# Gated attention and mixer-MLP kernel: W1 stored twice and split a step later, q and k written 16 dimensions outermost with two of three writes on ACT's queue, x and Wv issued earlier

## The chip, the core and the metric

The program runs on one core of a Trainium2 chip. The metric is the device time of one execution in microseconds. A measurement of this kernel can tell a change of about 1% from none.

## What is computed

x is 2048 tokens of 512 features in float32. Two branches are mixed by a gate per token:

```python
g = sigmoid((x * gate_w).sum(-1))
q, k, v = heads(x @ wqkv)                       # 32 heads of 16
p = softmax(where(0 <= i - j < 256, q k^T / 4, -1e9))
a = (p v) @ wo
b = gelu(layernorm(x) @ w1 + b1) @ w2 + b2      # 512 -> 1792 -> 512
out = g * a + (1 - g) * b
```

## The kernel before, in words

Every product in float32 accuracy is made of three fast products: an operand is split into h (a rounded copy, made by ACT in `copy`, line 98) and l (the rest, made by DVE or POOL in `lo_part`, line 95), and PE adds h h, l h and h l.

The program is written out in the order in which each engine runs it. SyncE (SP) issues all DMAs but one, in that order, and so do the compute engines with their instructions. `after(k, fn)` puts a piece of work k ticks later, and `tick()` runs what is due. Tiles called `t` come from one ring of raw buffers (12 in the first stage, 8 in the second); a new one waits until the last reader of the old one is done. Each DMA takes the next of eight semaphores in turn and waits until the DMA that had it last, eight issues earlier, has landed.

Stage 1 (to about 204 us) has 48 units, one a tick. A q/k unit (`qk_unit`, line 206) makes 128 rows of q or k, eight heads of 16 dimensions, for one of four chunks of 512 tokens: 12 matmuls into one of four PSUM banks, h by ACT, l by DVE, and three writes to HBM (line 222), h twice and l once, into a layout of 50 rows a head. A v unit (`v_unit`, line 225) makes 128 tokens of v and leaves them in SBUF. The first units are the q and k of heads 0 to 7 for chunks 0 to 2 (six units), then two v units, the q and k for chunk 3, and so on. The table `at(n, fn)` (lines 425 to 452) says before which unit the loads of x's chunks 2 and 3, of Wv (four tiles, `load_wv`), the gap rows (`gaps`, line 160), and the stacks of q and k for the first pair group are issued, and when the loaded tiles are split.

Stage 2 (about 204 to 757 us) runs over 8 groups p of four heads and 16 key blocks kb; one such step is one tick. A step makes the scores of a key block (`st_pair`: PE line 294, two exps by ACT line 296, masks by POOL line 298), the maxima for the group that comes next (`s_pair`: PE line 252, DVE lines 261 and 262), and in every other step the product with v (`pv`, PE line 309). Between these, `fill` puts matmuls of the first MLP layer (`mlp1_unit`, PE line 498), by a quota of 2.7 a half step. An MLP job is one tile of W1 (128 of the 1792 columns) with one half of the tokens. W1 has 14 such tiles; when the second job of tile f ends, `load_w1(f + 3)` issues the load of the next one:

```python
raws = [t2(), t2()]
for j, raw in enumerate(raws):
    sp.dma_start(raw, view(w1, [0, 2], [KT * 128, 64], [1, C], off=f * 64 * KT * 128 + j * C))
```

The 64 rows of W1 are needed in both halves of the 128 partitions, since two matmuls of 64 rows run side by side. `hi` (two copies on ACT) comes two ticks after the issue, `lo` (two subtractions, on DVE for the first three tiles, on POOL after) three ticks after. The first three tiles are loaded around the head of the stage, beside the second half of the normalised y (`load_y(1, 2, 1)`).

Stage 3 (from about 757 us) makes the second MLP layer (line 675) and the output projection (line 654).

Of the kernel before, what the change touches and what calls it, by code (L numbers as in the profile page):

```python
# [19 lines left out]
S = 2048  # L20
D = 512
H = 32
DH = 16
F = 1792
DT = D // 128
KT = D // 64
FT = F // 128
C = 512
NCH = S // C
NB = S // 128  # L30
NG = 4
HG = H // NG
# [11 lines left out]
def gated_mix_kernel(ctx, tc: tile.TileContext, xt, x2, wqk, wv, wo, xa, gw, w1, w2, b1, b2, out):  # L44
    nc = tc.nc
    dve, act, pool, pe, sp = nc.vector, nc.scalar, nc.gpsimd, nc.tensor, nc.sync
# [18 lines left out]
    def get(key, tag, bufs, shape, dt=F32):  # L65
        return left[key].tile(list(shape), dt, name=nm(tag), tag=tag, bufs=bufs)
# [3 lines left out]
    def t2(dt=F32, shape=(128, 512)):  # L70
        return get("work", "t", nt[0], shape, dt)
# [10 lines left out]
    def ps(tag, shape=(128, 512)):  # L82
        return left["psum"].tile(list(shape), F32, name=nm("ps_" + tag), tag=tag, bufs=banks[tag])
# [4 lines left out]
    def view(t, *ap, off=0):  # L88
        return bass.AP(tensor=t.tensor, offset=t.offset + off, ap=[list(x) for x in ap])

    def f32(t):
        return t.bitcast(F32)

    def lo_part(lo, src, hi, eng=dve):
        eng.tensor_tensor(out=lo, in0=src, in1=f32(hi), op=ALU.subtract)  # L95

    def copy(dst, src):
        act.activation(dst, src, AF.Copy)  # L98
# [4 lines left out]
    def after(k, fn):  # L103
        todo.setdefault(step[0] + k, []).append(fn)
# [34 lines left out]
    def x8():  # L139
        return get("x", "x8", 8, (128, 2048), F32R)  # L140

    def wt():
        return get("work", "w", 20, (128, 512), F32R)
# [16 lines left out]
    def gaps(g):  # L160
        for t in range(2):
            sp.dma_start(f32(view(qkd[g, t], [50 * S, HG], [S, 2], [1, S], off=48 * S)), f32(ks[0][112:128]))
# [15 lines left out]
    def load_wv(dt):  # L178
        raw = t2()
        sp.dma_start(raw, wv[dt])  # L180

        def rest():
            h, l = wt(), wt()
            copy(h, raw)
            lo_part(l, raw, h)
            wvs.append((h, l))

        return rest

    def load_x(c):  # L190
        raws = []
        for dt in range(DT):
            raws.append(t2())
            sp.dma_start(raws[dt], xt[c, :, dt * C:(dt + 1) * C])

        def rest(first=None):
            h, l = x8(), x8()
            for dt in range(DT):
                a, b = h[:, dt * C:(dt + 1) * C], l[:, dt * C:(dt + 1) * C]
                copy(a, raws[dt])  # L200
                lo_part(b, raws[dt], a, dve if c < 2 else pool)
                if dt == 0 and first:
                    first()
            xh.append(h)
            xl.append(l)

        return rest

    def qk_unit(g, t, c):
        d = qkd[g, t]  # L210
        o = ps("d")
        wh, wl = wq[g, t]
        n = 0
        for a, b in ((wh, xh[c]), (wl, xh[c]), (wh, xl[c])):
            for dt in range(DT):
                pe.matmul(o, a[:, dt * 128:(dt + 1) * 128], b[:, dt * C:(dt + 1) * C], start=n == 0, stop=n == 11)  # L216
                n += 1
        h, l = t2(F32R), t2(F32R)
        copy(h, o)
        lo_part(l, o, h)  # L220
        for k, s in ((0, h), (1 + t, h), (2 - t, l)):
            sp.dma_start(f32(view(d, [50 * S, HG], [S, DH], [1, C], off=k * DH * S + c * C)), f32(s))

    def v_unit(b):
        c, i = divmod(b, 4)
# [184 lines left out]
    wvr = []  # L410

    def QK(g, t, c):
        return lambda: qk_unit(g, t, c)
# [8 lines left out]
    def at(n, fn):  # L422
        plan.setdefault(n, []).append(fn)

    xs = {}
    at(0, lambda: xs.update({2: load_x(2)}))
    at(2, lambda: xs[2]())
    at(2, lambda: xs.update({3: load_x(3)}))
    at(4, lambda: xs[3]())
    for dt in range(DT):  # L430
        at(3 + dt // 2, lambda dt=dt: wvr.append(load_wv(dt)))
        at(5 + dt // 3, lambda dt=dt: wvr[dt]())
    for i in range(4):
        at(4 + i, lambda i=i: pool.memset(vs[:, 4 * i:4 * i + 4], 1.0))
    at(11, load_consts)
    for g in range(NG):
        at((1, 16, 20, 24)[g], lambda g=g: gaps(g))
    for c in range(NCH):
        at((4, 6, 8, 12)[c], lambda c=c: load_stacks(0, c))
    for i in range(NB):  # L440
# [23 lines left out]
    def load_w1(f):  # L464
        raws = [t2(), t2()]
        for j, raw in enumerate(raws):
            sp.dma_start(raw, view(w1, [0, 2], [KT * 128, 64], [1, C], off=f * 64 * KT * 128 + j * C))

        def hi():
            w1t[f] = get("work", "w1", 3, (128, 2, KT * 128), F32R)  # L470
            for j in range(2):
                copy(w1t[f][:, 0, j * C:(j + 1) * C], raws[j])

        def lo():
            for j in range(2):
                lo_part(w1t[f][:, 1, j * C:(j + 1) * C], raws[j], w1t[f][:, 0, j * C:(j + 1) * C], dve if f < 3 else pool)
            done.add(("w", f))

        after(2, hi)
        after(3, lo)  # L480

    jobs = [(0, 0), (1, 0), (0, 1), (1, 1)] + [(f, cp) for f in range(2, FT) for cp in range(2)]
    load_w1(0)
    load_y(1, 2, 1)
    after(1, lambda: load_w1(1))
    after(3, lambda: load_w1(2))

    def mlp1_unit(f, cp):
# [77 lines left out]
    for p in range(8):  # L566
        for kb in range(NB):
# [16 lines left out]
            if p == 7:  # L584
# [4 lines left out]
                if kb == 14:  # L589
                    for fn in ready:  # L590
                        fn()
                    t = x8()
# [93 lines left out]
    def item(n):  # L686
        return seq[n] if n < len(seq) else (0, -1)

    for n in range(len(seq)):
        tick()  # L690
        for k in (range(2, 4) if n == 0 else (n + 3,)):
            c, f = item(k)
# [4 lines left out]
        c, f = item(n + 1)  # L697
# [7 lines left out]
        c, f = seq[n]  # L705
# [11 lines left out]
def build():  # L717
    nc = bacc.Bacc("TRN2", target_bir_lowering=False, num_devices=1)

    def inp(name, shape):  # L720
        return nc.dram_tensor(name, list(shape), F32, kind="ExternalInput").ap()

    args = [inp("in_xt", (NCH, 128, DT * C)), inp("in_x2", (2, 128, KT * C)), inp("in_wqk", (NG, 2, 128, DT * 128)), inp("in_wv", (DT, 128, D)),
            inp("in_wo", (DT, 128, D)), inp("in_xa", (NB, 128, D)), inp("in_gw", (D,)),
            inp("in_w1", (FT, 64, KT * 128)), inp("in_w2", (FT, 128, D)), inp("in_b1", (128, FT)), inp("in_b2", (D,))]
    out = nc.dram_tensor("out", [NB, 128, D], F32, kind="ExternalOutput").ap()
    with tile.TileContext(nc) as tc:
        gated_mix_kernel(tc, *args, out)
    if not nc.is_finalized():
        nc.finalize()  # L730
    return nc
# [26 lines left out]
```

## Time and profile before

| | |
|---|---|
| median of 3 runs | 984.24 us (977.64 to 984.25) |
| the profiled execution | 978.83 us |
| its span | 977.1 us |
| PE (matmuls) busy | 775.8 us, 79% of the span |
| DVE busy | 516.1 us, 53% |
| ACT busy | 373.8 us, 38% |
| POOL busy | 303.0 us, 31% |
| mean granted TensorE clock | 0.896 of 2.4 GHz |

Times in the profile count from the start of the span. The busy times are means over stages with different limits, so a wait is read in its stage. A name such as `t<-in_w` is the tile written and the tensor read, with trailing digits left out (`in_w` is both `in_w1` and `in_w2`). "DMA" rows run from the issue to the landing.

### The profile page before, as it was taken

To read this page: it belongs to the slowest core of one execution; us is meant where nothing else is said; L and a number is where in the kernel's file an instruction comes from. 1 tells how busy PE (TensorE), PEld (TensorE's weight loads), DVE (VectorE), ACT (ScalarE), POOL (GpSimd) and SP (SyncE) were. 2 spreads that over 40 slices of the span, in tenths; PEclk is the share of its full clock that TensorE was granted. 3 is DMA by queue.
4 is the path that set the end of the run, shared out by engine and by line. 5 is a ranking of instruction groups with operands and counts; after the bars stand their busy time and mean duration, and the time that the engine had idled before them with its cause. 6 is when DMAs were issued, how large, how long until landed. Compare 5 with 4: busy or idle time off the path is not lost.

```text
span 977.1 us, 14415 instructions
## 1 busy us (share of the span) xinstructions
PE 775.8 (79%) x4832; PEld 534.6 (55%) x4832; DVE 516.1 (53%) x1087; ACT 373.8 (38%) x573; POOL 303.0 (31%) x597
## 2 busy tenths in 40 slices
PE   7498989914685669587696686876999699999998
PEld 5275657602453345354353454543556487888886
DVE  3126775602684347365384464654673566455544
ACT  4221112313553445354453454544556443222222
POOL 7500001702553435344363354443556000000000
PEclk9698989956797789797797988987999799999999
DMA  6776656633322233233223323332332755444442
GB/s 213 258 239 227 201 199 198 209 124 119 106 102 96 93 98 110 89 126 110 92 84 119 111 84 115 114 113 91 117 92 73 244 162 177 136 143 136 151 130 91
DMA packets 94741, 134.15 MB, mean 137 GB/s; under 512 B 13132, under 2 KB 38732, under 8 KB 94540
## 3 DMA queue, kind: packets, MB, share of 16 engines
q1 hardware_dynamic: 94524, 132.97, 41.4%
q8 instruction: 39, 0.64, 0.3%
q14 instruction: 34, 0.28, 0.1%
q10 hardware_dynamic: 144, 0.26, 0.1%
HBM read 78.91 MB, written 54.28 MB: 136 GB/s over the span
## 4 chain that ended last, share of the span: by engine, by line
PE 46%; DMA 29%; DVE 9%; SPq 5%; ACT 4%; POOL 3%; issue 3%; ACTq 0%; DVEq 0%; POOLq 0%
DMA t<-in_w 16%; PE ps_a L675 14%; PE ps_d L498 10%; PE ps_x L309 7%; PE ps_d L216 4%; PE ps_o L654 4%; PE ps_x L294 3%; PE ps_x L252 3%; DMA t<-in_xa 3%; DMA qk<-t 3%; DVE mx L262 2%; PE ps_d L231 2%; DVE ps_x L261 2%; ACT p L296 2%; DMA hp<-t 1%
## 5 line engine op out<-in xcount | busy, mean ns | idle before, releaser
L498 PE MATMUL ps_d<-x,w 64*128 64x512 f32 x1344 | 257.3, 424 | 21.1 <-ACT w L98 11.7
L298 POOL TENSOR_SCALAR_AFFINE_SELECT p<-p 128x256 f32<-128x256 f32 x480 | 188.0, 420 | 231.7 <-ACT p L296 228.1
L296 ACT ACTIVATE p<-ps_x 128x768 f32<-128x768 f32 (+2 forms) x256 | 192.9, 770 | 77.4 <-PE ps_x L294 63.0
L252 PE MATMUL ps_x<-k,q 62*128 62x384 f32 (+5 forms) x512 | 102.0, 380 | 109.2 <-ACT p L296 92.6
L261 DVE COPY_PREDICATED ps_x<-tri,ps_x 128x256 f32<-128x256 uint8 x224 | 94.9, 424 | 168.6 <-PE ps_x L252 168.0
L498 PEld LDWEIGHTS ps_d<-x,w 64*128 64x128 f32 x1344 | 146.3, 203 | 40.9 <-ACT w L98 12.8
L262 DVE TENSOR_REDUCE mx<-ps_x 128x2 f32<-128x512 f32 x224 | 155.1, 692 | 7.7
L675 PE MATMUL ps_a<-x,t 128*128 128x512 f32 x648 | 155.0, 397 | 0.1
L675 PEld LDWEIGHTS ps_a<-x,t 128*128 128x128 f32 x648 | 121.8, 188 | 30.2 <-DVE t L541 0.5
L252 PEld LDWEIGHTS ps_x<-k,q 48*128 48x128 f32 (+1 forms) x512 | 55.1, 197 | 138.2 <-ACT p L296 108.7
L294 PE MATMUL ps_x<-q,k 50*128 50x384 f32 (+5 forms) x512 | 105.4, 391 | 28.4 <-ACT p L296 22.3
L309 PE MATMUL ps_x<-p,v 128*32 128x384 f32 (+2 forms) x1024 | 101.3, 514 | 15.8 <-DVE mx L262 6.7
L294 PEld LDWEIGHTS ps_x<-q,k 50*128 50x128 f32 (+1 forms) x512 | 56.2, 197 | 94.2 <-issue 35.8
L216 PE MATMUL ps_d<-x,w 128*128 128x512 f32 x384 | 101.1, 420 | 6.1 <-ACT w L98 6.1
L216 PEld LDWEIGHTS ps_d<-x,w 128*128 128x128 f32 x384 | 75.8, 200 | 27.2 <-ACT w L98 6.1
L537 ACT ACTIVATE t<-t,b1s 128x512 f32<-128x512 f32 x56 | 39.5, 721 | 117.0 <-DMA t<-hp 111.4
L98 ACT ACTIVATE w<-t 128x512 fp32r<-128x512 f32 x40 | 25.2, 629 | 139.2 <-DMA t<-in_w 116.8
L98 ACT ACTIVATE t<-ps_x 128x512 f32<-128x512 f32 (+1 forms) x59 | 33.8, 573 | 112.1 <-PE ps_x L309 109.4
L309 PEld LDWEIGHTS ps_x<-p,v 128*32 128x32 f32 x1024 | 30.9, 116 | 67.9 <-issue 34.2
L95 DVE TENSOR_TENSOR t<-t,t 128x512 fp32r<-128x512 f32 x70 | 48.5, 692 | 30.8 <-ACT t L98 26.0
L319 POOL TENSOR_TENSOR t<-t,t 128x256 f32<-128x256 f32 x51 | 37.5, 736 | 87.4 <-ACT t L98 87.4
L231 PE MATMUL ps_d<-w,x 128*128 128x512 f32 x192 | 52.6, 425 | 14.1 <-ACT w L98 14.1
(66 smaller groups left out, 562.6 us busy)
## 6 DMA issues: line engine op xcount, KB each, us to landing
qk<-t SPq DMA_DIRECT2D x96, 256.0 KB
hp<-t SPq DMA_DIRECT2D x56, 256.0 KB
t<-hp SPq DMA_DIRECT2D x56, 256.0 KB
k<-qk SPq DMA_DIRECT2D x64, 196.0 KB
q<-qk SPq DMA_DIRECT2D x64, 196.0 KB
t<-in_w SPq DMA_DIRECT2D x42, 256.0 KB
osc<-t SPq DMA_DIRECT2D x64, 128.0 KB
t<-in_xt SPq DMA_DIRECT2D x16, 256.0 KB
```

The costliest lines, as they stand in the source:

```text
L98: act.activation(dst, src, AF.Copy)
L216: pe.matmul(o, a[:, dt * 128:(dt + 1) * 128], b[:, dt * C:(dt + 1) * C], start=n == 0, stop=n == 11)
L231: pe.matmul(o, x[:, a:a + 128], wvs[dt][k], start=n == 0, stop=n == 11)
L252: pe.matmul(o[:, e, :n], qs[pr][r:k, qb * 128:qb * 128 + 128], ks[pr][r:k, t0:t0 + n], start=True, stop=True)
L261: dve.copy_predicated(o[:, :, :128], tri, o[:, :, 256:384])
L262: dve.tensor_reduce(m, o[:, :, :256], mybir.AxisListType.X, ALU.max)
L294: pe.matmul(o[:, e, :w], ks[pr][r:k, kb * 128:kb * 128 + 128], qs[pr][r:k, kb * 128:kb * 128 + w], start=True, stop=True)
L296: act.activation(pt[:, :, :w], o[:, :, :w], AF.Exp, scale=0.25)
L298: pool.affine_select(out=pt[:, :, a:a + 128], in_=pt[:, :, a:a + 128], pattern=[[0, 2], [sgn, 128]], base=b, channel_multiplier=-sgn, comp ...
L309: pe.matmul(a[32 * h:32 * h + 32, odd * 128:odd * 128 + w], vs[:, kb, v:v + 32], pt[:, h, :w], start=not odd, stop=odd == 1, skip_group_ch ...
L498: pe.matmul(o[e], w[r:r + 64, k, kt * 128:kt * 128 + 128], y[r:r + 64, a:a + C], start=n == 0, stop=n == 23)
L675: pe.matmul(accs[c][b], x[:, b * 128:(b + 1) * 128], w, start=f == 0 and n == 0, stop=f == FT - 1 and n == 2)
```

## The change

W1 is handed over with its 64 rows repeated, so that a load reads 128 rows straight; the split of a W1 tile comes one tick later (3 and 4 ticks after the issue). The columns of the q and k weights are put in the order dimension, head, so that a unit's rows come out as 16 dimensions of 8 heads, and the writes have the 16 dimensions outermost; the bytes land where they did. The two writes of h are issued by ACT right behind its copy, the write of l by SP one tick later. x's chunk 3 is issued before unit 0 instead of 2, Wv's four tiles before units 1 and 2 instead of 3 and 4, and split before units 3 and 4 instead of 5 and 6; the gap rows of the first heads come a unit later.

```diff
-        for k, s in ((0, h), (1 + t, h), (2 - t, l)):
-            sp.dma_start(f32(view(d, [50 * S, HG], [S, DH], [1, C], off=k * DH * S + c * C)), f32(s))
+        for k in (0, 1 + t):
+            act.dma_start(f32(view(d, [S, DH], [50 * S, HG], [1, C], off=k * DH * S + c * C)), f32(h))
+        after(1, lambda: sp.dma_start(f32(view(d, [S, DH], [50 * S, HG], [1, C], off=(2 - t) * DH * S + c * C)), f32(l)))
...
-    at(2, lambda: xs.update({3: load_x(3)}))
+    at(0, lambda: xs.update({3: load_x(3)}))
     at(4, lambda: xs[3]())
     for dt in range(DT):
-        at(3 + dt // 2, lambda dt=dt: wvr.append(load_wv(dt)))
-        at(5 + dt // 3, lambda dt=dt: wvr[dt]())
+        at(1 + dt // 2, lambda dt=dt: wvr.append(load_wv(dt)))
+        at(3 + dt // 2, lambda dt=dt: wvr[dt]())
...
-        at((1, 16, 20, 24)[g], lambda g=g: gaps(g))
+        at((2, 16, 20, 24)[g], lambda g=g: gaps(g))
...
         for j, raw in enumerate(raws):
-            sp.dma_start(raw, view(w1, [0, 2], [KT * 128, 64], [1, C], off=f * 64 * KT * 128 + j * C))
+            sp.dma_start(raw, w1[f, :, j * C:(j + 1) * C])
...
-        after(2, hi)
-        after(3, lo)
+        after(3, hi)
+        after(4, lo)
...
-            inp("in_w1", (FT, 64, KT * 128)), inp("in_w2", (FT, 128, D)), inp("in_b1", (128, FT)), inp("in_b2", (D,))]
+            inp("in_w1", (FT, 128, KT * 128)), inp("in_w2", (FT, 128, D)), inp("in_b1", (128, FT)), inp("in_b2", (D,))]
...
     w1 = B_w1.reshape(KT, 64, FT, 128).transpose(2, 1, 0, 3).reshape(FT, 64, KT * 128)
+    w1 = np.concatenate([w1, w1], axis=1)
...
-        "in_wqk": f(A_wqkv[:, :2 * D].reshape(DT, 128, 2, NG, 128).transpose(3, 2, 1, 0, 4).reshape(NG, 2, 128, DT * 128)),
+        "in_wqk": f(A_wqkv[:, :2 * D].reshape(DT, 128, 2, NG, HG, DH).transpose(3, 2, 1, 0, 5, 4).reshape(NG, 2, 128, DT * 128)),
```

Line numbers from 222 on are higher by one after the change.

On SP near the start, before; `qk` is the q/k tensor in HBM, `in_xt` x, `in_wv` Wv:

```order
L194 DMA t_41_223<-in_xt 128x512
L194 DMA t_42_225<-in_xt 128x512
L194 DMA t_43_227<-in_xt 128x512
L194 DMA t_44_229<-in_xt 128x512
L222 DMA qk0_0_65<-t_46_244 8x16x512 x2
L222 DMA qk0_0_65<-t_47_245 8x16x512
L180 DMA t_48_251<-in_wv 128x512
L180 DMA t_49_253<-in_wv 128x512
L222 DMA qk0_1_66<-t_51_268 8x16x512 x2
L222 DMA qk0_1_66<-t_52_269 8x16x512
L180 DMA t_55_285<-in_wv 128x512
L180 DMA t_56_287<-in_wv 128x512
```

On SP near the start, after:

```order
L194 DMA t_33_171<-in_xt 128x512
L194 DMA t_34_173<-in_xt 128x512
L194 DMA t_35_175<-in_xt 128x512
L194 DMA t_36_177<-in_xt 128x512
L223 DMA qk0_0_65<-t_39_193 16x8x512
L180 DMA t_40_199<-in_wv 128x512
L180 DMA t_41_201<-in_wv 128x512
L223 DMA qk0_1_66<-t_44_217 16x8x512
L180 DMA t_47_233<-in_wv 128x512
L180 DMA t_48_235<-in_wv 128x512
```

Wv stood behind x's last chunk and the writes of four units (those of the first two stand above the piece shown); now the last chunk of x comes first of all, and one write of l from each of the first two units stands ahead of Wv.

On ACT near the start, after; before, these rows are the same without the two DMA rows, and the copies of x's third chunk (`x8_39` there) follow the second copy of `ps_d` at once:

```order
L98 ACTIVATE t_38_192<-ps_d_37_179 128x512
L222 DMA qk0_0_65<-t_38_192 16x8x512 x2
L98 ACTIVATE t_43_216<-ps_d_42_203 128x512
L222 DMA qk0_1_66<-t_43_216 16x8x512 x2
L98 ACTIVATE x8_45_223<-t_29_163 128x512
L98 ACTIVATE x8_45_223<-t_30_165 128x512
```

Each of the 32 q/k units now has two DMA issues in ACT's order between one copy out of PSUM and the next.

On ACT in stage 2 at the fourth tile of W1, before; `p` is an exp, `t<-ps_d` the copy that ends an MLP job, before the W1 load of that job, and `w1<-t` the copies of the loaded tile:

```order
L296 ACTIVATE p_405_2179<-ps_x_406_2180 128x2x256
L296 ACTIVATE p_405_2179<-ps_x_408_2194 128x2x256
L98 ACTIVATE t_411_2205<-ps_d_385_2045 128x512
L98 ACTIVATE t_415_2223<-ps_x_414_2214 128x512
L296 ACTIVATE p_416_2229<-ps_x_417_2230 128x2x128
L296 ACTIVATE p_416_2229<-ps_x_421_2252 128x2x128
L98 ACTIVATE w1_423_2270<-t_409_2201 128x512
L98 ACTIVATE w1_423_2270<-t_410_2202 128x512
```

The same place on ACT after:

```order
L98 ACTIVATE t_418_2239<-ps_d_387_2054 128x512
L297 ACTIVATE p_421_2258<-ps_x_422_2259 128x768
L297 ACTIVATE p_421_2258<-ps_x_426_2282 128x768
L98 ACTIVATE t_429_2308<-ps_x_428_2299 128x256
L297 ACTIVATE p_430_2312<-ps_x_431_2313 128x768
L297 ACTIVATE p_430_2312<-ps_x_433_2328 128x768
L98 ACTIVATE w1_438_2351<-t_416_2235 128x512
L98 ACTIVATE w1_438_2351<-t_417_2236 128x512
```

Between the end of the job that issues the load and the copies of the tile stand the exps of two steps instead of one.

## Rows read from the trace of the kernel before

**Rows 1.** The page, part 4: the chain that ended last, by line.
```profile
DMA t<-in_w 16%; PE ps_a L675 14%; PE ps_d L498 10%; PE ps_x L309 7%; PE ps_d L216 4%; PE ps_o L654 4%; PE ps_x L294 3%; PE ps_x L252 3%; DMA t<-in_xa 3%; DMA qk<-t 3%; DVE mx L262 2%; PE ps_d L231 2%; DVE ps_x L261 2%; ACT p L296 2%; DMA hp<-t 1%
```

**Rows 2.** Windows: length, busy (instructions) of PE, PEld, DVE, ACT, POOL; PEclk, DMA share, GB/s.
```profile
26.00:50.00 24.00, 9.91 (x29) 6.66 (x28) 3.92 (x6) 6.78 (x12) 12.55 (x8) 0.64 0.74 259
50.00:196.65 146.65, 131.79 (x544) 98.33 (x542) 88.97 (x213) 31.85 (x57) 21.48 (x16) 0.95 0.64 212
204.30:290.10 85.80, 49.73 (x352) 29.80 (x354) 42.04 (x83) 35.56 (x54) 31.82 (x63) 0.74 0.32 102
290.10:674.90 384.80, 278.46 (x2286) 171.38 (x2282) 205.33 (x464) 170.07 (x255) 170.73 (x375) 0.87 0.31 103
757.00:977.10 220.10, 208.38 (x900) 165.31 (x892) 120.31 (x202) 70.22 (x111) 2.12 (x5) 0.97 0.48 152
```

**Rows 3.** Waits, whole span: waiter, waited for; us in total, times, longest.
```profile
ACT w L98 <- DMA t<-in_w: 116.8, 28, 8.5
```

**Rows 4.** Timeline 307.5 to 326, SP and ACT: start, us, instruction, idle before.
```profile
309.99 1.09 SPq L467 DMA_DIRECT2D t<-in_w  x2
...
312.61 1.51 ACT L296 ACTIVATE p<-ps_x 128x768 f32<-128x768 f32 x2
317.76 0.63 ACT L98 ACTIVATE w<-t 128x512 fp32r<-128x512 f32 x1 [3.65 <-DMA t<-in_w]
323.02 0.63 ACT L98 ACTIVATE w<-t 128x512 fp32r<-128x512 f32 x1 [4.63 <-DMA t<-in_w]
```

**Rows 5.** Windows as in rows 2, three short stretches.
```profile
317.00:322.50 5.50, 0.00 (x0) 0.00 (x0) 0.00 (x0) 0.63 (x1) 0.00 (x0) 0.76 0.13 50
187.00:200.00 13.00, 8.27 (x37) 6.01 (x35) 4.40 (x8) 3.64 (x7) 5.45 (x4) 0.88 0.52 198
314.50:316.50 2.00, 1.49 (x14) 0.80 (x10) 1.71 (x3) 0.00 (x0) 0.53 (x2) 1.00 0.90 338
```

**Rows 6.** Windows of line 296 (the exps) alone: length, ACT busy (count), PEclk, DMA, GB/s.
```profile
683.20:736.20 53.00, 24.28 (x33) 1.00 0.35 109
290.10:674.90 384.80, 127.92 (x171) 0.87 0.31 103
262.60:285.50 22.90, 9.73 (x12) 1.00 0.33 109
204.30:290.10 85.80, 23.28 (x30) 0.74 0.32 102
```

**Rows 7.** Chain that ended last, in order of time, to 212 us: start, us, what.
```profile
0.80 4.07 DMA t<-in_xt
...
89.57 8.37 DMA t<-in_xa
...
200.03 5.46 DMA qk<-t
```

**Rows 8.** Groups by line and form: busy us, mean ns, idle before.
```profile
L95 POOL TENSOR_TENSOR w<-t,w 128x512 fp32r<-128x512 f32 x22 | 27.8, 1282 | 0.0
```

**Rows 9.** Timeline 0 to 60, as rows 4.
```profile
16.50 5.05 POOL L95 TENSOR_TENSOR x<-t,x 128x512 fp32r<-128x512 f32 x4 [2.67 <-ACT x L98]
17.80 4.74 SPq L222 DMA_DIRECT2D qk<-t  x3
...
27.89 1.32 SPq L180 DMA_DIRECT2D t<-in_wv  x2
...
32.17 1.49 SPq L180 DMA_DIRECT2D t<-in_wv  x2
...
36.44 1.45 PE L231 MATMUL ps_d<-w,x 128*128 128x512 f32 x2 [9.94 <-ACT w L98]
...
41.84 0.80 PE L231 MATMUL ps_d<-w,x 128*128 128x512 f32 x1 [3.94 <-ACT w L98]
```

**Rows 10.** Timeline 196 to 205, as rows 4.
```profile
204.31 0.81 ACT L296 ACTIVATE p<-ps_x 128x768 f32<-128x768 f32 x1 [8.06 <-DMA qk<-t]
```

## The prediction, made before the changed kernel ran

> **What bounds the kernel now.** I read the chain that ended last first: the largest DMA share in it is the load of W1 into its raw buffers [rows 1]. Then busy time by stretch [rows 2]. The last 220.10 us have PE busy for 208.38 and the change leaves them alone. The attention and first-MLP stage is the place: from 290.10 to 674.90 PE works 278.46 of 384.80 us. The table of waits says who is late: ACT waited 28 times for W1, 116.8 us in all, up to 8.5 us each [rows 3]. One such wait in order of time [rows 4]: SP issues both halves of a W1 tile at 309.99, ACT is done with the exps of its step at 314.12 (312.61 + 1.51), and the copies of the halves start at 317.76 and 323.02. ACT runs in order, so the exps behind the copies are late, and with them PE. Meanwhile [rows 5] from 317 to 322.5 the DMA engines are 0.13 busy and move 50 GB/s, which is two of sixteen; just before, under the writes of the MLP's results, they stood at 0.90 and 338 GB/s. So W1 is slow because nearly all of the engines do nothing. The q and k writes at the end of the first stage show the same at half: 0.52 busy and 198 GB/s for 13 us, eight of sixteen. The source agrees with both: W1's read has an outermost dimension of 2, the q/k write one of 8.
>
> A row shows the busy share, not the cause. The Trainium skill (DMA: Bandwidth & Descriptors, "Why a DMA increments its semaphore by 16 and not by 1") says that a DMA of SP or ACT runs on the largest number of engines up to 16 that divides the slowest dimension of both sides, and its rules name a leading broadcast of c copies as confined to c. The trace agrees at 2 and at 8; no row shows it for a write with 16 outermost. By the rule the time is the forecast below, without it the 912 of the second rival.
>
> **W1 in the steady stretch, 290.10 to 674.90.** It holds 171 exps, two a step, so 85 steps [rows 6], and eleven of the fourteen W1 tiles. Between 683.20 and 736.20 no W1 comes in and all else goes on: 33 exps, so 16 steps, in 53.00 us, 3.31 us a step, at a granted clock of 1.00 (2.4 GHz) where the long stretch has 0.87. If no copy waits any more, 85 x 3.31 = 281 us. Does it wait? The copies now stand one step further back, so ACT comes to them about 3.5 + 3.3 = 6.8 us after the second half was issued (that was near 310.5, and ACT stood free at 314.1). A 256 KB load of 128 rows landed in 4.07 us at the quiet start and in 8.37 us at the worst of the first stage [rows 7], both from the chain, and 50 GB/s turning into the 338 of rows 5 takes the two halves from 10.5 us of moving to 1.6. I take landed in time; at the worst 1.6 us are left per tile. What the clean stretch lacks is the split itself: two ACT copies of 0.63 us (rows 4) and two POOL subtractions of 1.28 us [rows 8]. They cost between nothing, beside PE, and 3.8 us in line; I take 1.3, near the ACT part, since the masks on POOL have a step of slack before PE's PV reads them. 11 x 1.3 = 14. So 384.8 - 281 - 14 = 90 us gained; bounds 384.8 - 281 = 104 and, with 3.8 + 1.6 each, 44.
>
> **W1 at the head of that stage, 204.30 to 290.10.** 30 exps, 15 steps in 85.80 us, clock 0.74; it holds three W1 tiles and the second half of y. The stretch 262.60 to 285.50 has y but no W1: 12 exps, six steps in 22.90 us, 3.8 a step. 15 x 3.8 = 57, and 3 x 1.3 = 4 for the splits: 61, a gain of 24. Bounds: 36 at 3.31 a step, and 0 if it is DVE's work on y, beside which it splits W1, that sets this stretch. The matmuls of the MLP also begin one step later, and the order has twelve more of them in the drain at the end: 278.46 / 2286 = 0.12 us each, 1 us lost.
>
> **The first stage.** Three things. Wv first: PE waits 9.94 and 3.94 us for it [rows 9], since its loads stand on SP behind x's last chunk and behind writes, issued at 27.89 and 32.17. Now the first two stand behind one write of l, the last two behind a second one and behind POOL's first two subtractions for x's third chunk (16.50 + 2 x 5.05 / 4 = 19.0). Issued near 19.8 and landing in 4.07 to 8.37 us, they are there at 24 to 28; ACT's copies follow those of x's last chunk, so PE, ready at 36.44 - 9.94 = 26.5, starts near 29. Gain 11 of 13.9; bounds 9 and 13.9. Most of the stretch from 26 to 50 ran at 1.2 GHz (granted 0.64): 29 matmuls at 9.91 / 29 = 0.34 us against 131.79 / 544 = 0.24 later, so 2 us more. Second, from 50 to 196.65 PE idles 146.65 - 131.79 = 14.9 us; the chain names loads and q/k writes there. With the writes on all engines I take 5; bounds 0 and 13. Third, the end: the exp that opens the next stage waits 8.06 us for the last q/k writes [rows 10]; issued behind two writes less and moving at twice the rate, they should end 4 us sooner; bounds 0 and 7.5. Sum 22; bounds 9 and 36.
>
> What the move of h's writes adds: 64 DMA issues in ACT's order, at 0.55 us (W1's issue in rows 4) to 1.58 us (4.74 / 3, rows 9) 35 to 101 us. From 50 to 196.65 alone ACT has 146.65 - 31.85 = 115 us free (rows 2). I put it at nothing, since four PSUM banks let PE run four units ahead; if that cover goes, ACT's copy out of PSUM is what is late, and PE behind it. l's write, a unit later, is read by no one before the unit in which its chunk's stack loads are due. x's last chunk and the gaps are only two units earlier and one later on SP; PE needs the first at unit 8 and the second at unit 13, so neither has a price. W1 written twice in HBM moves the bytes that were read twice before.
>
> **The sum.** The profiled execution took 978.83 us (span 977.1). 90 + 24 - 1 + 22 = 135, so 844; the runs' median, 984.24, is 5 us above it, of which I give 1: 845. Its own range: with the steady term half way to its lower bound (23 us) 868; with all three terms half way to their upper bounds (14 + 12 + 14, halved) 825.
>
> **Rivals.** (1) PE is no longer held by W1, but POOL, ACT and DVE don't follow at 3.31. For it: 3.8 a step where DVE has y to do. Against: the clean stretch is sixteen steps long. Then 85 x 0.5 = 43 us less: 888. (2) The change doesn't do what it says: W1 is slow for a reason other than its outermost dimension, and still lands 12 us after issue. Then only the step later counts: 3.3 us of each stall, 11 x 3.3 = 36, 8 at the head, 22 before: 912. Against it are the 0.13 of rows 5. (3) The first stage gains nothing, since ACT, with 35 to 101 us of issues, gives back what SP and Wv gain: 845 + 22 = 867. The Trainium skill speaks for this one (same page, "Issuing engines are not separate DMA queues"): issuing from more engines saves only the sequencer's time. (4) Slower. Each DMA of the program shares one of eight semaphores in turn with the one eight before it and waits until that has landed; on SP this held loads, on ACT it now holds the copies that free PSUM. Place: the 32 q/k units. Price: if each of the two writes in a unit waits a whole landing (5.46, rows 7), a unit takes 0.6 + 2 x (5.46 + 0.55) = 12.6 us and the stage 32 x 12.6 = 403 instead of 204: 978.83 + 199 - 113 = 1065. It decides where the waits pass 113 / 64 = 1.8 us a write beyond ACT's slack of 115 / 64 = 1.8: some 3.6 us at each. Against it: a landing halves when sixteen engines move it, and eight DMAs are then rarely in flight.
>
> **How the numbers follow.** Forecast 0.75, rivals 0.1, 0.04, 0.08 and 0.03. Two in ten may lie outside: the range takes in rival 3 and goes up to the edge of rival 1, 886, and down to 820, a little below the forecast's own range. A change of more than 1%, about what a measurement of this kernel can tell from none, is 10 us: all cases but the fourth are faster. Faster 0.95, same 0.02, slower 0.03.
>
> **What would show it.** Right: ACT's wait for W1 near zero in the table of waits, DMA share near 1 for a microsecond or two after a W1 issue, steps of 3.3 to 3.6 us from the fourth tile on at a clock near 1.00, first V matmul near 29 us, first exp near 182. Wrong: W1 waits of some us left (rival 2, or a landing over 7 us); the clock at 1.00 and steps of 3.8 with PE waiting for POOL or DVE (rival 1); ACT waiting for DMAs ahead of its q/k copies with PE idle before 200 us (rivals 3, 4).

## The result and the profile after

The changed kernel takes 828.28 us (median of 4 runs, 826.69 to 829.89) where the kernel before takes 982.59 in the same comparison: ratio 0.8437, 95% interval 0.8399 to 0.8475. Its profiled execution took 826.69 us with a span of 825.0, against 978.83 and 977.1. Medians leave out runs more than 1.5% above the fastest of the same kernel.

The windows of the changed kernel, cut where [rows 2] are cut: first stage (three pieces), head of the second stage up to its sixteenth step, the next 85 steps, and the last stage. Columns as in [rows 2].

```profile
0.00:26.00 26.00, 17.87 (x59) 12.36 (x59) 8.32 (x13) 11.24 (x18) 17.51 (x20) 1.00 0.83 286
26.00:50.00 24.00, 20.58 (x76) 16.06 (x77) 6.76 (x9) 8.69 (x16) 13.60 (x9) 0.86 0.89 263
50.00:169.50 119.50, 116.44 (x513) 87.13 (x511) 85.75 (x212) 30.23 (x54) 22.60 (x16) 1.00 0.82 255
169.50:227.90 58.40, 45.58 (x350) 25.43 (x348) 41.90 (x82) 34.22 (x53) 31.62 (x63) 0.91 0.47 149
227.90:521.10 293.20, 263.90 (x2272) 162.65 (x2268) 204.78 (x462) 167.41 (x253) 170.44 (x375) 0.97 0.42 133
...
615.00:825.00 210.00, 204.55 (x864) 164.34 (x864) 115.30 (x195) 63.57 (x100) 0.00 (x0) 0.98 0.46 149
```

Read the first column against [rows 2]. The first exp of the second stage now comes at 169.5 us, not 204.3: 34.8 gained. The head takes 58.4 us instead of 85.8: 27.4. The 85 steps take 293.2 instead of 384.8: 91.6, or 3.45 us a step instead of 4.53. From there to the end 303.9 us against 302.2: 1.7 lost. The sum is 152.1, all that lies between the two spans. In the 85 steps PE's busy time fell only from 278.46 to 263.90; its idle time fell from 106.3 to 29.3.

The chain that ended last, by line (page, part 4), answers to [rows 1]:

```profile
PE ps_a L676 19%; PE ps_d L499 14%; PE ps_x L310 10%; PE ps_d L216 8%; PE ps_o L655 5%; DMA q<-qk 5%; PE ps_x L295 5%; PE ps_x L253 5%; PE ps_d L232 4%; DMA qk<-t 3%; DVE mx L263 2%; ACT p L297 2%; DMA t<-in_w 2%; ACT t L98 2%; DVE ps_x L262 1%
```

W1's load has gone from the head of the list (16%) to 2%, and PE's own work leads. One W1 tile in the timeline of SP and ACT, to be held against [rows 4]; the lines have moved by one:

```profile
301.94 0.92 SPq L468 DMA_DIRECT2D t<-in_w  x2
...
310.03 1.66 ACT L297 ACTIVATE p<-ps_x 128x768 f32<-128x768 f32 x2
...
311.58 1.14 ACT L98 ACTIVATE w<-t 128x512 fp32r<-128x512 f32 x2
```

The two copies run back to back behind the exps, with no wait in front of them. The wait of [rows 3] is gone from the table of waits. The two microseconds behind the issue, as a window beside the 0.13 and 50 GB/s of [rows 5], and one W1 landing in the chain:

```profile
302.40:304.40 2.00, 0.72 (x5) 0.21 (x2) 1.86 (x6) 1.09 (x2) 1.33 (x4) 1.00 0.75 212
```

```profile
229.75 4.07 DMA t<-in_w
```

The first stage, from the timeline of the start: the first V matmul, the next wait of PE, and ACT's longest wait there.

```profile
18.55 0.60 ACT L98 ACTIVATE t<-ps_d 128x512 fp32r<-128x512 f32 x1 [5.92 <-DMA qk<-t]
...
29.28 0.63 PE L232 MATMUL ps_d<-w,x 128*128 128x512 f32 x2
...
33.19 7.95 PE L232 MATMUL ps_d<-w,x 128*128 128x512 f32 x22 [3.28 <-ACT w L98]
```

So PE comes to V at 29.28, not at 36.44 [rows 9], and waits 3.28 us once. ACT's wait of 5.92 us for a write of q or k looks like what the fourth rival feared, but it does not come from ACT's queue. In the experiments below every kernel with the earlier loads has it, wherever the writes are issued: 6.19 us with the earlier loads alone, 5.16 with h's writes back on SP. In the kernels without them no such wait passes 1.4 us there. What does come from ACT's queue are waits of its copies of v later in the stage, which are gone with h's writes on SP. The table of waits of the changed kernel:

```profile
ACT v L98 <- DMA qk<-t: 6.9, 2, 4.0
ACT v L98 <- DMA q<-qk: 6.1, 1, 6.1
```

PE waits for no copy of v more than 0.7 us.

### The profile page after: what moved, and what is told of

Read it like the earlier page. It is cut to its first block, busy times and chain, and to the rows that moved or that the text cites. A ratio compares the mean times of both kernels' runs of the same rounds, so it can differ in the third digit from the quotient of the medians.

```text
span 825.0 us, 14409 instructions
## 1 busy us (share of the span) xinstructions
PE 749.9 (91%) x4832; PEld 517.4 (63%) x4832; DVE 516.0 (63%) x1087; ACT 370.6 (45%) x573; POOL 304.6 (37%) x597
## 4 chain that ended last, share of the span: by engine, by line
PE 68%; DMA 12%; DVE 7%; ACT 5%; issue 3%; POOL 2%; SPq 1%; ACTq 1%; DVEq 0%
PE ps_a L676 19%; PE ps_d L499 14%; PE ps_x L310 10%; PE ps_d L216 8%; PE ps_o L655 5%; DMA q<-qk 5%; PE ps_x L295 5%; PE ps_x L253 5%; PE ps_d L232 4%; DMA qk<-t 3%; DVE mx L263 2%; ACT p L297 2%; DMA t<-in_w 2%; ACT t L98 2%; DVE ps_x L262 1%
## 5 line engine op out<-in xcount | busy, mean ns | idle before, releaser
L499 PE MATMUL ps_d<-x,w 64*128 64x512 f32 x1344 | 249.4, 408 | 14.9 <-DVE t L509 7.7
L499 PEld LDWEIGHTS ps_d<-x,w 64*128 64x128 f32 x1344 | 140.7, 192 | 34.1 <-DVE t L509 12.6
L253 PE MATMUL ps_x<-k,q 48*128 48x384 f32 (+5 forms) x512 | 97.6, 361 | 20.0 <-DMA q<-qk 9.2
L310 PE MATMUL ps_x<-p,v 128*32 128x384 f32 (+2 forms) x1024 | 96.8, 497 | 14.1 <-ACT p L297 4.9
L295 PE MATMUL ps_x<-q,k 50*128 50x384 f32 (+5 forms) x512 | 103.2, 380 | 6.6 <-DVE mx L263 2.0
L216 PE MATMUL ps_d<-x,w 128*128 128x512 f32 x384 | 98.3, 408 | 8.3 <-ACT w L98 6.4
L216 PEld LDWEIGHTS ps_d<-x,w 128*128 128x128 f32 x384 | 72.6, 192 | 29.8 <-ACT w L98 6.4
L253 PEld LDWEIGHTS ps_x<-k,q 62*128 62x128 f32 (+1 forms) x512 | 52.7, 187 | 48.6 <-ACT p L297 26.6
L95 DVE TENSOR_TENSOR t<-t,t 128x512 fp32r<-128x512 f32 x70 | 48.5, 692 | 29.9 <-ACT t L98 26.7
L98 ACT ACTIVATE t<-ps_d 128x512 fp32r<-128x512 f32 (+1 forms) x60 | 35.7, 596 | 54.1 <-PE ps_d L216 37.4
L232 PE MATMUL ps_d<-w,x 128*128 128x512 f32 x192 | 50.4, 414 | 3.3 <-ACT w L98 3.3
```

What stands on the lines that cost most here:

```text
L232: pe.matmul(o, x[:, a:a + 128], wvs[dt][k], start=n == 0, stop=n == 11)
L253: pe.matmul(o[:, e, :n], qs[pr][r:k, qb * 128:qb * 128 + 128], ks[pr][r:k, t0:t0 + n], start=True, stop=True)
L295: pe.matmul(o[:, e, :w], ks[pr][r:k, kb * 128:kb * 128 + 128], qs[pr][r:k, kb * 128:kb * 128 + w], start=True, stop=True)
L310: pe.matmul(a[32 * h:32 * h + 32, odd * 128:odd * 128 + w], vs[:, kb, v:v + 32], pt[:, h, :w], start=not odd, stop=odd == 1, skip_group_ch ...
L499: pe.matmul(o[e], w[r:r + 64, k, kt * 128:kt * 128 + 128], y[r:r + 64, a:a + C], start=n == 0, stop=n == 23)
```

## The experiments

All ratios are to the kernel before on the same chip. The column of V is the first matmul with Wv. These are the landmarks of the profiled executions, in us, from the starts of the exps and the span (step 15 and step 100 count from the first exp's step, two exps each):

```
                first V  first exp  to step 15  to step 100  to the last  to the end
before            36.4     204.3       85.8        384.8         88.3       213.9
changed           29.3     169.5       58.4        293.2         89.2       214.6
W1 rows           34.9     204.0       59.9        289.5         84.9       213.2
split later       35.6     202.1       80.4        368.4         96.7       213.6
both of W1        36.3     207.3       59.9        296.9         89.0       213.6
four DMAs         36.6     212.6       61.2        301.1         91.3       213.7
stage 1, all      29.5     169.8       84.7        392.1         87.6       214.1
stage 1, order    28.5     198.1       92.3        387.0         87.1       213.6
stage 1, 16       29.9     167.8       85.3        387.6         87.9       213.4
h on SP           27.2     163.0       59.9        299.8         87.1       213.3
eight outermost   32.3     211.9       62.6        293.8         88.3       213.2
two layouts       30.8     168.4       60.0        291.4         85.2       214.2
SP, split sooner  27.5     163.5       59.1        287.2         85.2       213.2
 and y alternate  27.9     162.7       62.1        287.1         85.4       213.7
```

Each row is one execution. The kernel before and the three below it that share its first stage (W1 rows, split later, both of W1) have their first exp at 202.1 to 207.3, so differences of some 5 us there mean little. The three with h on SP lie within 0.8 us of each other.

**W1 in 128 rows alone.** The first theory: an outermost dimension of 2 put W1 on two of sixteen DMA engines, and this is the second stage's loss.

```diff
-            sp.dma_start(raw, view(w1, [0, 2], [KT * 128, 64], [1, C], off=f * 64 * KT * 128 + j * C))
+            sp.dma_start(raw, w1[f, :, j * C:(j + 1) * C])
...
+    w1 = np.concatenate([w1, w1], axis=1)
```

> The kernel before with W1 laid out twice and read in 128 rows; the split stays two steps after the issue, and the first stage is as before. Theory: the load was slow because its outermost dimension of 2 put it on two of sixteen DMA engines; on all of them a half lands about 4 us after the issue, when ACT is done with the exps it has ahead of the copies, so a W1 tile still costs some 0 to 2 us: nearly all of the second stage's 117 us are gained, 982.6 to about 870 to 885, and the waits of ACT for W1 are under 2 us each. Rival (the step later does it, the load is slow for another reason): waits of 4 to 8.5 us stay, time above 960.

Measured: 857.73 us, ratio 0.8727 (0.8686 to 0.8769), a gain of 125. The table of waits:

```profile
ACT w L98 <- DMA t<-in_w: 11.0, 7, 2.9
```

The theory holds, and the gain is larger than it said: seven waits are left, 11 us in all. One of them, at the head of the stage, reaches PE, which waits 2.5 us for the copy.

**The split a step later alone.**

```diff
-        after(2, hi)
-        after(3, lo)
+        after(3, hi)
+        after(4, lo)
```

> The kernel before with the split of W1 one step later alone; W1 still read as 2 x 64 rows. Theory: the second half still lands some 12 us after the issue, so each of the fourteen stalls is only shorter by the step of 3.3 us: 14 x 3.3 = 46, so about 937 (930 to 950), and ACT's waits for W1 come to 40 to 75 us instead of 116.8. Rival (the copies only stood too early, and one step covers them): about 865 to 880 with the waits near zero.

Measured: 964.04 us, ratio 0.981 (0.9753 to 0.9867). The table of waits:

```profile
ACT w L98 <- DMA t<-in_w: 76.9, 21, 6.3
```

The waits fell by 40 us, as the theory said, but the time by only 19 and not by 46. Its rival falls altogether. The time of a wait in the table is not the price of it. PE's waits for ACT's exps ahead of line 252 fell from 92.6 to 32.7 us, but PE now waits for loads of q, for which it waited 1.4 us before:

```profile
PE ps_x L252 <- DMA q<-qk: 28.8, 11, 9.3
...
PE ps_x L294 <- DMA q<-md: 24.0, 4, 6.9
```

With W1 read in 128 rows as well, the first of these is 10.5 us and the second is gone. So the slow load, no longer waited for by ACT, was felt through other loads instead.

**Both edits of W1.** The two diffs above together.

> The kernel before with both edits of W1 and the first stage as before. Theory: the gain of the second stage between the two traces (27 us in its first fifteen steps, 92 in the next 85, 2 lost later) needs nothing of the first stage's edits: 982.6 - 117 = 865 (860 to 871). Rival (the faster q and k writes or the earlier start also feed the second stage): 875 or more.

Measured: 864.99 us, ratio 0.8792 (0.8756 to 0.8827): the number of the theory. The second stage's gain stands by itself. But it is 7 us above the layout alone, so the later split costs something. The steady stretch of the two, layout alone first:

```profile
264.00:553.50 289.50, 259.50 (x2280) 160.64 (x2276) 205.48 (x462) 168.18 (x255) 170.79 (x375) 0.99 0.43 137
```

```profile
267.30:564.20 296.90, 267.53 (x2270) 165.01 (x2268) 204.66 (x462) 167.63 (x254) 170.74 (x375) 0.95 0.42 131
```

PE's idle time is the same (30.0 and 29.4 us); the 8 us are in its busy time, at a granted clock of 0.95 instead of 0.99.

**W1 once in the input, read by two DMAs of 64 rows.** Does the outermost dimension count, or that the bytes lie twice in HBM?

```diff
-            sp.dma_start(raw, view(w1, [0, 2], [KT * 128, 64], [1, C], off=f * 64 * KT * 128 + j * C))
+            for e in range(2):
+                sp.dma_start(raw[64 * e:64 * e + 64], w1[f, :, j * C:(j + 1) * C])
```

> W1 stays once in the input, 64 rows, and each half is read by two DMAs of 64 rows to the upper and the lower 64 partitions, issued one behind the other; the split is a step later; the first stage is as before. Theory: what counts is the outermost dimension of the DMA (64 instead of 2), not that the bytes lie twice in HBM: within 1% of the kernel with the double layout, about 865; two more issues on SP a tile cost nothing. Rival (the two readers of the same HBM rows hold each other up): waits of several us stay and the time is above 900.

Measured: 879.56 us, ratio 0.894 (0.8909 to 0.8971). The table of waits:

```profile
ACT w L98 <- DMA t<-in_w: 2.6, 2, 1.9
```

So the outermost dimension is what counted, and 104 of the 118 us come without any second copy in HBM. It is 14.6 us slower than the double layout, though. In the landmarks 4 of these lie in the steady stretch and 5 before the first exp, where the two programs read the same in the source and kernels differ by as much without a reason; what the rest is made of stays open. The Trainium skill (DMA: Bandwidth & Descriptors, "Rules for kernel authors") advises one transfer of 128 partitions instead of two to disjoint halves, since both share the same engines. The 14.6 us agree, and the 104 show that two halves are still far better than one leading dimension of 2.

**The first stage's edits alone.** The changed kernel's q and k layout, ACT's queue, l's write and the earlier loads, with W1 as before (the diff of the change without W1's lines).

> The kernel before with all edits of the first stage (q and k written 16 dimensions outermost, h from ACT's queue, l a unit later, x and Wv issued earlier) and W1 as before. Theory: the first exp comes 35 us earlier, as between the two traces (204.3 to 169.5), and the stalls for W1 stay: 982.6 - 35 = 948 (943 to 953). Rival (the gain of the first stage is partly taken back by W1's first tiles, which wait for the bandwidth the quicker start needs): above 955.

Measured: 944.92 us, ratio 0.9626 (0.9583 to 0.9669), first exp at 169.8. This is within the theory's range, and the two stages add up: 37 and 118 make 155, where the change gained 154.

**Of these, the earlier loads alone.**

```diff
-    at(2, lambda: xs.update({3: load_x(3)}))
+    at(0, lambda: xs.update({3: load_x(3)}))
...
-        at(3 + dt // 2, lambda dt=dt: wvr.append(load_wv(dt)))
-        at(5 + dt // 3, lambda dt=dt: wvr[dt]())
+        at(1 + dt // 2, lambda dt=dt: wvr.append(load_wv(dt)))
+        at(3 + dt // 2, lambda dt=dt: wvr[dt]())
...
-        at((1, 16, 20, 24)[g], lambda g=g: gaps(g))
+        at((2, 16, 20, 24)[g], lambda g=g: gaps(g))
```

> The kernel before with x's last chunk and Wv issued earlier, and nothing else. Theory: this is the start of the first stage, the 13.9 us in which PE waits for Wv and the matmuls there that ran at 1.2 GHz: first V matmul near 29 us, gain 11 to 15, about 970. Rival (the q and k writes, still on eight DMA engines, hold the earlier loads up): a gain under 6, above 976.

Measured: 980.90 us, ratio 0.9979 (0.9953 to 1.0006): nothing. The first V matmul did come at 28.5, and yet it is nothing. The first 26 us, the kernel before and then this one:

```profile
0.00:26.00 26.00, 19.87 (x71) 15.32 (x72) 9.19 (x14) 11.71 (x19) 18.00 (x20) 1.00 0.66 216
```

```profile
0.00:26.00 26.00, 18.42 (x62) 13.38 (x63) 8.22 (x14) 12.37 (x21) 17.73 (x20) 1.00 0.79 263
```

The windows after that, of this kernel:

```profile
26.00:50.00 24.00, 20.19 (x84) 15.24 (x82) 6.45 (x9) 6.28 (x12) 13.84 (x8) 1.00 0.63 204
```

```profile
50.00:198.10 148.10, 127.34 (x500) 94.42 (x500) 88.04 (x212) 30.73 (x56) 21.78 (x16) 0.88 0.63 212
```

At 50 us PE is 46 matmuls ahead of the kernel before (146 against 100). Then 500 matmuls take 148.1 us, where 544 took 146.65 before [rows 2]: PE's idle time there goes from 14.9 to 20.8 us and its clock from 0.95 to 0.88. The idle time was not removed but moved. The 6 us that are left of the lead at the first exp go at the head of the second stage, where the second half of W1's third tile is there for ACT at 245.65 in the one and 245.39 in the other.

**Of these, the layout of q and k alone**, all writes still on SP and at once.

```diff
-        for k, s in ((0, h), (1 + t, h), (2 - t, l)):
-            sp.dma_start(f32(view(d, [50 * S, HG], [S, DH], [1, C], off=k * DH * S + c * C)), f32(s))
+        for k in (0, 1 + t):
+            sp.dma_start(f32(view(d, [S, DH], [50 * S, HG], [1, C], off=k * DH * S + c * C)), f32(h))
+        sp.dma_start(f32(view(d, [S, DH], [50 * S, HG], [1, C], off=(2 - t) * DH * S + c * C)), f32(l))
```

(with the same order of columns in the input of Wq and Wk)

> The kernel before with q and k written 16 dimensions outermost, all three writes still on SP and at once. Theory: the writes take half as long and SP's loads behind them land sooner; PE's idle time from 50 us on (14.9 us) and the wait for the last writes (8.1) fall: gain 10 to 20, 963 to 973, and the DMA share in the last part of the stage rises above 0.52. Rival (the writes were hidden, and what waited was only issued late): a gain under 4.

Measured: 943.05 us, ratio 0.9601 (0.9562 to 0.964): all of the first stage's gain, twice what was expected. The windows:

```profile
26.00:50.00 24.00, 18.22 (x61) 13.38 (x60) 6.89 (x10) 8.37 (x14) 11.94 (x8) 0.79 0.97 309
50.00:167.80 117.80, 116.69 (x516) 87.50 (x514) 85.99 (x209) 29.30 (x53) 23.40 (x16) 1.00 0.80 256
```

From 50 us on PE idles 1.1 us, and V starts at 29.9 with Wv still issued at 24.0 and not at 14. So the layout of the writes is what held the first stage. Per engine nothing got faster, by an estimate from the busy shares: 198 GB/s at a share of 0.52 [rows 5] are 24 GB/s for each of the 8.3 engines at work, 309 at 0.97 are 20 for each of 15.5. What rose is the number of engines at work. How full the eight were can be estimated from the kernel before, in its transfers from 50 to 196 us:

```profile
DMA packets 16817, 30.91 MB, mean 212 GB/s; under 512 B 2102, under 2 KB 2102, under 8 KB 16711
...
qk<-t SPq DMA_DIRECT2D x75, 256.0 KB
```

75 writes are 19.7 MB; at the 198 GB/s that eight engines moved [rows 5] they alone take 99 us. If the other 11.2 MB lie evenly on sixteen engines, the eight carry 5.6 MB more, 28 us: an estimate of 127 us out of 146. A mean share of 0.64 over sixteen engines would then hide eight that were nearly full; no view here lists the engines one by one.

**The changed kernel with h's writes back on SP.**

```diff
-            act.dma_start(f32(view(d, [S, DH], [50 * S, HG], [1, C], off=k * DH * S + c * C)), f32(h))
+            sp.dma_start(f32(view(d, [S, DH], [50 * S, HG], [1, C], off=k * DH * S + c * C)), f32(h))
```

> The changed kernel with the two writes of h back on SP; l's write stays a unit later, all else as changed. Theory: of the first stage's 35 us only what SP's order costs is lost, 64 issues of 0.5 to 0.6 us in front of its loads: 2 to 8 us, so 830 to 836. Rival (ACT's queue was the point of the edit: h's writes stand behind SP's loads there and PE waits for PSUM): 10 us or more, above 838. Third: ACT was held by its own issues, and without them the time falls below 825.

Measured: 821.92 us, ratio 0.8355 (0.8314 to 0.8396). The third of the expectations holds: ACT's queue gave nothing and cost some 6 us. The start shows it:

```profile
0.00:26.00 26.00, 18.59 (x67) 14.04 (x68) 9.42 (x16) 13.57 (x24) 18.12 (x21) 1.00 0.87 295
26.00:50.00 24.00, 21.76 (x91) 16.35 (x89) 7.38 (x9) 7.49 (x15) 13.41 (x8) 1.00 0.92 279
50.00:163.00 113.00, 111.31 (x489) 83.07 (x488) 85.33 (x209) 27.92 (x51) 22.22 (x16) 1.00 0.82 260
```

By 50 us PE has done 158 matmuls instead of 135; 23 at 111.31 / 489 = 0.23 us are 5.2 us. ACT still waits 5.16 us for a write of q or k, but what comes behind is sooner. In the changed kernel ACT's own issues stand between its copies, and the copies of Wv's last two tiles start at 32.52:

```profile
28.07 2.32 ACTq L222 DMA_DIRECT2D qk<-t  x2
...
30.43 2.19 ACT L98 ACTIVATE x<-t 128x512 fp32r<-128x512 f32 x4 [2.39 <-issue]
...
32.52 1.13 ACT L98 ACTIVATE w<-t 128x512 fp32r<-128x512 f32 x2
```

With h on SP they start at 26.96, and PE's wait of 3.28 us in V is down to 0.39:

```profile
17.83 0.60 ACT L98 ACTIVATE t<-ps_d 128x512 fp32r<-128x512 f32 x1 [5.16 <-DMA qk<-t]
...
26.96 1.15 ACT L98 ACTIVATE w<-t 128x512 fp32r<-128x512 f32 x2
```

**The changed kernel with eight outermost again**, everything else as changed: what are the moves worth without the layout?

```diff
-            act.dma_start(f32(view(d, [S, DH], [50 * S, HG], [1, C], off=k * DH * S + c * C)), f32(h))
+            act.dma_start(f32(view(d, [50 * S, HG], [S, DH], [1, C], off=k * DH * S + c * C)), f32(h))
```

(l's write and the input of Wq and Wk likewise)

> The changed kernel with q and k written 8 dimensions outermost, as before: h still from ACT's queue, l a unit later, x and Wv first. Theory: the first stage was bound by the eight DMA engines that took all q and k writes, so without the layout the other edits give nothing back: 828 + 35 = 863 (857 to 870), first exp near 200, and the PE idle time that has gone from the start stands between 50 and 196 us. Rival (the moved issues and ACT's queue are worth half of it): first exp near 185, time near 845.

Measured: 874.16 us, ratio 0.8894 (0.8863 to 0.8924), first exp at 211.9. The moves alone do harm: 9 us more than with W1's edits and nothing moved (0.8756 to 0.8827). Its window from 50 us on has the figures of the kernel before, or worse:

```profile
50.00:196.00 146.00, 123.48 (x475) 90.70 (x474) 80.80 (x199) 25.60 (x47) 16.21 (x13) 0.89 0.64 205
```

**The two layouts alone**, no issue moved: the diffs of W1's rows and of the q and k layout together.

> The two layouts alone: W1 read in 128 rows (split two steps after the issue, as before) and q and k written 16 dimensions outermost; no issue moved, nothing on ACT's queue. Theory: the two layouts are the whole of it: 982 - 126 - 39 = 817 (812 to 822), below the changed kernel's 828, since the later split cost 7 and ACT's queue 5. Rival (the moved issues are worth something once the writes are quick, and the later split pays when the loads of both compete): 828 or more.

Measured: 819.61 us, ratio 0.8337 (0.8308 to 0.8365): 163 us gained where the two gave 125 and 39 apart. They are the whole of it, and 9 us better than the change.

**h on SP and the split sooner.**

```diff
-            act.dma_start(f32(view(d, [S, DH], [50 * S, HG], [1, C], off=k * DH * S + c * C)), f32(h))
+            sp.dma_start(f32(view(d, [S, DH], [50 * S, HG], [1, C], off=k * DH * S + c * C)), f32(h))
...
-        after(3, hi)
-        after(4, lo)
+        after(2, hi)
+        after(3, lo)
```

> The changed kernel with h's writes back on SP and W1's split two steps after the issue instead of three; x and Wv stay first, l's write stays a unit later. Theory: the split a step sooner gives 7 us here as it did without the first stage's edits (857.7 against 865.0): 823.4 - 7 = 816 (812 to 820), at a granted clock of about 0.99 in the steady stretch against 0.95. Rival (the 7 us were chance in the clock of two executions): 821 to 825.

Measured: 814.46 us, ratio 0.8281 (0.8253 to 0.8308), the best here: 14 us below the changed kernel. It is 5 us below the two layouts, with the first exp at 163.5 instead of 168.4: the earlier loads and l's later write (not tried apart) are worth something once the writes are quick, where the earlier loads alone were worth nothing before. So the rival of the two layouts was right in part. And the split a step sooner again gives 7 us. Ten microseconds of PE in the kernel with the split later (first) and sooner:

```profile
313.00:323.00 10.00, 8.56 (x60) 0.83 0.26 95
```

```profile
313.00:323.00 10.00, 9.49 (x82) 1.00 0.30 108
```

With the split later, steps of 5.8 to 9.2 us stand at the same places in three kernels (the changed one, the one with h on SP and the one with W1's edits alone): the seventh and the eleventh of the third head group, the fifteenth of the fifth. In each a first-MLP unit ends, right behind a step that closes a group of four maxima on DVE. The chain of the changed kernel at one of these, with a PV of sixteen matmuls before it and its own:

```profile
314.39 1.43 PE ps_x L310 x16
...
320.37 0.70 DVE t L509
321.12 1.65 PE ps_d L499 x7
322.76 2.72 PE ps_x L310 x16
```

The PV that took 1.43 us takes 2.72: nearly twice as long, as at the lower of the clock's two levels, 1.2 GHz, and the granted clock is 0.50 from 322.0 to 325.4. PE had waited for the copies out of its banks just before, 0.33 us for ACT's and 0.79 for DVE's. With the split sooner such ends of units come too, at other steps, but from the third head group on these last 3.6 to 5.3 us, at a granted clock of 1.00 in every ten microseconds. Why the one order lets the clock fall and the other doesn't wasn't settled.

**And y's work alternating between DVE and POOL.**

```diff
-                eng = dve if cp else pool
+                eng = dve if cp and kt % 2 else pool
```

> As the kernel with h's writes on SP and the split two steps after the issue, and the subtraction and product of y's second half alternate between DVE and POOL instead of DVE alone. Theory: DVE sets the first fifteen steps of the second stage (chain of waits), so eight products and subtractions less there take 2 to 5 us off, 811 to 814. Rival: POOL takes 1.3 us for what DVE does in 0.8 and its masks come late: no change or slower, 816 or more.

Measured: 818.43 us, ratio 0.8317 (0.8287 to 0.8347): no gain, and the head took 62.1 us instead of 59.1. POOL's slower work on y is not better placed than DVE's.

## Why the prediction was right, and where it was not

**The steady stretch: right.** Forecast 90, measured 91.6. The W1 copies no longer wait, the clean stretch's 3.31 us a step plus the split is what remains: 3.45. The split was put at 1.3 us a tile; (293.2 - 281) / 11 is 1.1. That the sum came within 2 us is partly luck: the 1.1 holds the clock's loss (0.97 against the clean stretch's 1.00), and at the clock of 0.99 of the layout alone (289.5 - 281) / 11 is 0.8. The layout alone removes nearly all of ACT's wait, so the cause was the one named. The Trainium skill's rule that opened the second paragraph of the prediction (DMA: Bandwidth & Descriptors, "Why a DMA increments its semaphore by 16 and not by 1") agrees with the trace at 2 (0.13) and at 8 (0.52) and now at 16: with that layout alone the engines are 0.97 busy from 26 to 50 us.

**The head: right.** Forecast 24, measured 27.4; 3.9 us a step, where the stretch with y but no W1 gave 3.8.

**The split a step later: wrong sign.** It was priced at 1 us for the drain of the MLP, and as what let W1 land in time. The landing shown takes 4.07 us; the step was not needed, and it costs 7 us, in lower clock (857.73 to 864.99 without the first stage's edits, 814.46 to 821.92 with them; in the first pair the two intervals just overlap). The 91.6 of the steady stretch hold a part of this loss: with the layout alone it took 289.5, a gain of 95.

**The first stage: too small, and for the wrong reason.** This is the step that failed: forecast 22, measured 34.8, and with 3 us at the head nearly the whole of the miss of 17 us. It was built of "Wv first" (11 and 2 of clock), the idle time from 50 us on (5, bounds 0 and 13) and the last writes (4). The first was read from PE's waits of 9.94 and 3.94 us for Wv [rows 9] as a matter of SP's order. The order alone gave nothing, the layout alone gave 39 us. PE's wait at V was only the first place at which the writes' few DMA engines came to be felt; with the order alone the wait came later. The middle was sized at a third of its bound: its idle time fell from 14.9 to 3.1 us. And its clock, 0.95 before, went to 1.00: 131.79 / 544 less 116.44 / 513, times 544, is 8 us that no term held. The end was put at half of its bound, and its wait is gone whole, 8.06 us [rows 10] against 0.56:

```profile
169.52 2.21 ACT L297 ACTIVATE p<-ps_x 128x768 f32<-128x768 f32 x3 [0.56 <-PE ps_x L295]
```

As an estimate, the 34.8 are 8 at the start (135 matmuls done at 50 us, not 100, at 0.24), 12 of idle time, 8 of clock and 7.5 at the end.

**ACT's 64 issues: put at nothing, cost 6.** They took 41.5 us in all, near the lower of the two figures given, 35. The cover named, four PSUM banks, holds from 50 us on, where PE idles 3.1 us, and 1.7 with h on SP. At the start it does not cover: ACT has x's and Wv's copies in the same order as its issues, and V waits for them. The third rival (867) fell with its time, since the gain was the layout's. Its argument on the issues is borne out: with the writes from SP the stage is no slower, its first exp at 163.0 against 169.5. Beside that stands the Trainium skill's rule (DMA: Bandwidth & Descriptors, "Issuing engines are not separate DMA queues") that another issuing engine saves sequencer time alone. The 163.0 agree.

**The rivals.** The first (DVE and POOL hold 3.8 a step) is excluded by 3.45. The second (W1 slow for another reason, 912) is excluded by the wait's end; its price was off as well, since the step later alone gave 19 us and not 44. The fourth's mechanism shows, in three waits of ACT's copies of v of 6.1, 4.0 and 2.9 us, but the four PSUM banks cover them.

**The signs.** First V matmul 29.28 (29 announced), steps of 3.45 (3.3 to 3.6), clock 0.97 (near 1.00), W1's wait gone: as said. First exp 169.5, not 182; DMA share 0.75 behind a W1 issue, not near 1.

## What to carry to other kernels

A mean DMA share well below 1 can hide a few engines that are full: hold the share against how many engines each transfer's outermost dimension lets it use before you blame the order of the issues. Mend the layout first and measure it alone; here the two layouts gave 163 us, and of the moves made beside them the earlier ones on SP were worth 5 us only afterwards, and two cost 6 and 7. When a wait stands at a start, ask whether it would only come later: a kernel that does just that edit tells it.

## What the runs showed of the hardware

W1's transfers, which keep 0.13 of sixteen engines busy, two of them [rows 5], queue behind each other, and SP is held up in its issues as well. The timeline of the kernel before at the head of the second stage, where three W1 tiles come close together:

```profile
219.65 4.83 SPq L378 DMA_DIRECT2D t<-in_x  x2
...
224.52 5.85 SPq L467 DMA_DIRECT2D t<-in_w  x2
...
245.39 0.63 ACT L98 ACTIVATE w<-t 128x512 fp32r<-128x512 f32 x1 [5.10 <-DMA t<-in_w]
```

W1's six halves are there for ACT at 214.3, 219.7, 227.3, 232.5, 239.7 and 245.4, the two halves of each tile 5.3 to 5.7 us apart: 262 KB at 50 GB/s are 5.2 us. And two issues of SP take 4.8 to 5.9 us there, also that of x's load, where two of W1's took 1.09 in [rows 4].

A granted clock of 0.95 instead of 0.99 over 290 us, at the same idle time of PE, made 7 us of difference between two orders of the same work. The mean idle share did not tell which order would lose it.
